# Handing out dense steps by size, and weighing ahead of the parameters, in a fused state-space and dense-layer gradient

## The chip, the cores and the metric

One core of a Trainium2 chip runs the kernel in one launch. The metric is the device time of one execution in microseconds. The kernel before took 776.42 us in the median of three runs (769.07, 776.42, 781.49).

## The reference

A gate `g = sigmoid(u . gate_w)` mixes two branches of a sequence of 2048 rows and 448 channels in bf16. The first is a diagonal state-space model with 256 states in each channel, applied as a long convolution by FFT; the second a dense layer of width 1792 with a squared relu. The kernel returns the mixed output and the gradients of all fourteen parameters.

```python
def _A_ref(u, A_re, A_im, B_re, B_im, C_re, C_im, log_dt, Dskip):
    ...
    P = jnp.exp(logdA[:, :, None] * l[None, None, :])
    K = jnp.einsum("dn,dnl,dn->dl", Cc, P, dB).real
    ...
    Yf = Uf * Kf[None, :, :, :]          # rfft of length 2L of u and K
    y = irfft2(Yf)[..., :L] + u * Dskip
def _B_ref(x, w1, b1, w2, b2):
    h = jnp.einsum("bsd,df->bsf", x, w1) + b1
    r = jnp.where(h > zero, h, zero)
    return jnp.einsum("bsf,fd->bsd", r * r, w2) + b2
g = _sigmoid((x * gate_w).sum(-1, keepdims=True))
out = g * a + (1 - g) * b               # x = u for both branches
_out, _vjp = jax.vjp(_f, ...)           # and the gradients for grad_out
```

## The kernel before

The work goes through these stages. Line numbers are those of the kernel before.

First, input and its gradient G are loaded; U is transposed (L437), and the gate g and 1-g are found (L456 to L461). DA = g G is made (L463). Two first FFT stages (`fwd1`, L236 its matmuls, L210/L211/L220 copies out of PSUM, L244 stores to DRAM) turn U and then DA. Their blocks are staged in a ring of buffers: eight for the first, six for the second, eight blocks each.

Between and behind them stand: the parameters' work on DVE and ACT (L481 to L524: products with dt, an exponential at L512, sines at L519 and L520, a square at L521), which ends in the tables that the chains start from; the weighing DB = (1-g) G (L541, sixteen DVE instructions); the column sum over 1-g (matmuls L544, copy L554); and the gate product, sixteen DVE products DA*U into four slots (L548), each summed by a matmul with ones (L549, copy L551).

Then the second FFT stage. `spectra(q)` (q = 0 to 3) loads a quarter of each of the two transforms (L250), multiplies (`fwd2`, matmuls L260) and stores it (L965). `cmul` (L274 to L279, DVE) multiplies the two, and `inv1` (L296 its matmuls, L300 its stores) begins the way back. Four chains `powers` stand between them: each squares the state's complex factor eleven times over. A level is an ACT copy (L595), an ACT square (L604) and two DVE instructions (L605, L606) that need each other; L591 opens a chain, a store to `rec_d` (L609, on ACT's queue) closes it. The chains use two sets of buffers in turn.

The dense layer runs as a generator of 189 steps that the other stages draw from. `N_(n)` runs the next n steps. A list `cost` gives each a size. A column j of the first layer (14 columns) has four steps: `hidden` of half a column with `turn` (matmuls L661 and L664, relu copies L676, turns L688, squares L689), 24; `mul_1` (L697, copy L703), 19; and again both. After columns 1 and 2 stand four steps each of size 6, `turn_db`: ten transposes (L437), one copy (L710, on ACT for an even number and on DVE for an odd one) into one of two halves of a buffer, and its store (L711, to `DBT_d`). Within `spectra` and `inv1` each slot runs a number of steps: `FW` = (1, 1, 0, 1) behind the four parts of `fwd2`, `IV` = (2, 2) behind the two parts of `inv1`. With four steps run before, forty are done at the end of `spectra` and three `inv1`.

Up to there the order of each engine's instructions is a scheduler's, which may move instructions past one another. From `manual_schedule` on (L972) it is that of the program. There the last `inv1` and the y-tables take ten more steps, and steps are drawn until a product is complete. Then come fourteen periods of the state-space gradient, one for each 32 channels (lists of tokens, `PERIOD`). The token D draws steps until the sum of their sizes reaches an even share of what is left, so that the periods end with six steps left. Stores and loads of the dense layer's later part are held (`defer`) and released at the tokens LY and R, or when a buffer must be used again (`force`); L784 is the copy of the second layer's hidden gradient into one of three such buffers, L794 its store. DMA transposes (L1102) of the y-tables stand in SP's queue between them. A last stage of 148 us, FFTs of the kernel's gradient and the outputs, follows the periods.

Of the kernel before, what the change touches and what calls it, by code (L numbers as in the profile page):

```python
# [23 lines left out]
DT = 4  # L24
# [295 lines left out]
def kernel(ctx, tc, A_u, A_A_re, A_A_im, A_B_re, A_B_im, A_C_re, A_C_im, A_log_dt, A_Dskip,  # L320
# [46 lines left out]
    krow = np.array([p if p < 32 else p // 32 * 32 + (p % 16) * 2 + p // 16 % 2 if p < 64 else 64 + (p % 16) * 4 + p // 16 % 4 for p in range(P)])  # L367
    cs["F1K"] = np.zeros_like(cs["F1BD"])
# [93 lines left out]
    for t in range(LT):  # L462
# [4 lines left out]
             for homes in (((Fs, (0, 1792, 3584, 5376)), (RA, (10752, 12544)), (S1t[0], (0, 1792))), ((S1t[1], (0, 1792, 3584, 5376)), (S1t[0], (3584, 5376))))]  # L467
# [5 lines left out]
    nMI = const.tile([P, 256], bf16, name="nMI")  # L473
    S.mul(nMI[:], ct["MI"][:], -1.0)
    K.nMI = nMI
# [64 lines left out]
    for t in range(LT):  # L540
        V.tensor_scalar(out=DB[:, t, :], in0=G[:, t, :], scalar1=omg32[:, t:t + 1], scalar2=None, op0=ALU.mult)  # L541
    ps = K.ps("S", [P, 512])
    for t in range(LT):
        T_.matmul(ps[0:1, 0:D], lhsT=omg_b[:, t:t + 1], rhs=G[:, t, :], start=(t == 0), stop=(t == LT - 1))  # L544
    psg = K.ps("X", [P, 512])
    gu = K.t("st", [P, 4, D], bufs=2)
    for t in range(LT):
        V.tensor_tensor(out=gu[:, t % 4], in0=DA[:, t], in1=U[:, t], op=ALU.mult)  # L548
        T_.matmul(psg[0:1, 0:D], lhsT=ones_c[:], rhs=gu[:, t % 4], start=(t == 0), stop=(t == LT - 1))  # L549
    row9 = K.t("st", [P, 4, D], bufs=2)  # L550
    S.copy(row9[0:1, 0], psg[0:1, 0:D])  # L551
    G_.dma_start(out_9.rearrange("(o d) -> o d", o=1), row9[0:1, 0])
    row13 = K.t("rec", [1, D])
    S.copy(row13[:], ps[0:1, 0:D])  # L554
    G_.dma_start(out_13.rearrange("(o d) -> o d", o=1), row13[:])
# [59 lines left out]
    w1b = [SB[:, 8192 + 1024 * i:9216 + 1024 * i].rearrange("p (a f) -> p a f", a=DT) for i in range(2)]  # L615
# [33 lines left out]

    def load_w1(jp):  # L650
        b = w1b[jp % 2]
        G_.dma_start(b[:, 0:3], bass.AP(tensor=B_w1.tensor, offset=B_w1.offset + 256 * jp, ap=[[F, P], [P * F, 3], [1, 256]]))
        for h in range(2):
            G_.dma_start(b[64 * h:64 * h + 64, 3], bass.AP(tensor=B_w1.tensor, offset=B_w1.offset + 384 * F + 256 * jp, ap=[[F, 64], [1, 256]]))
# [66 lines left out]
    def first_layer():  # L721

        for jp in range(2):
            load_w1(jp)
# [219 lines left out]

    def D_(want):

        while done < total - TAILN and sum(cost[0:done + 1]) <= want:
            N_(1)
# [741 lines left out]
```

## Time and profile before

| what | value |
|---|---|
| median of three runs | 776.42 us |
| profiled execution, its own time | 771.82 us |
| its span | 769.9 us |
| granted TensorE clock, mean | 0.906 |
| busy: PE, DVE, ACT, POOL | 638.2, 566.7, 510.9, 174.6 us |
| DMA moved | 177.77 MB |

The span is what the profile's times count, from its start; the time of the execution has 1.9 us around it. PE's busy time counts matmuls as they overlap, and those at a lower clock are longer. All durations in the prediction come from this one execution. Where instructions of one engine follow each other without a pause, the profile's duration of one is longer than the distance of their starts, since they overlap; distances are used for sums.

### The profile page before, as it was taken

The numbers are of one execution on the slowest core, as the hardware profiler recorded it, in microseconds if no ns is written. First come the engines' busy times: TensorE is split into PE (matmuls) and PEld (weight loads), VectorE is DVE, ScalarE is ACT, GpSimd is POOL, SyncE is SP. The second block draws the span as 40 slices with busy tenths as digits, with TensorE's granted clock in tenths as the row PEclk, the third lists the DMA queues.
The fourth block names the chain that finished last, engine by engine and source line by source line (L and its number), as shares of the span: only waits on it lengthen the run. The fifth ranks groups of instructions, "written<-read, shape, count | busy, mean of one in ns | idle before, by whom it ended". The sixth has DMA issues, their size and how long they took to land.

```text
span 769.9 us, 20498 instructions
## 1 busy us (share of the span) xinstructions
PE 638.2 (83%) x8597; PEld 339.2 (44%) x8597; DVE 566.7 (74%) x932; ACT 510.9 (66%) x873; POOL 174.6 (23%) x296
## 2 busy tenths in 40 slices
PE   5958968779999888698999997998979987686666
PEld 2412322333456545355665654654636563433211
DVE  1397586775784549598898898698879868859474
ACT  2797958588785746477687677677725544498455
POOL 2152111112174101111211201102100332321543
PEclk9997967899999988889999999999989998799858
DMA  9898586746783995967977977999996976898995
GB/s 206 185 284 255 198 307 240 250 168 217 295 324 90 314 194 128 267 120 206 241 173 206 259 140 194 258 185 251 223 219 129 280 234 206 344 332 303 335 332 146
DMA packets 197115, 177.77 MB, mean 231 GB/s; under 512 B 121534, under 2 KB 174039, under 8 KB 196895
## 3 DMA queue, kind: packets, MB, share of 16 engines
q1 hardware_dynamic: 173823, 113.11, 59.5%
q0 software_dynamic: 15632, 44.48, 18.1%
q10 hardware_dynamic: 7568, 18.88, 6.6%
q8 instruction: 67, 1.10, 0.6%
q14 instruction: 25, 0.20, 0.1%
HBM read 83.95 MB, written 64.32 MB: 193 GB/s over the span
## 4 chain that ended last, share of the span: by engine, by line
PE 50%; ACT 15%; issue 13%; DMA 10%; DVE 7%; POOL 3%; SPq 2%; POOLq 0%; ACTq 0%; DVEq 0%
PE psN L901 9%; PE psN L661 6%; PE psN L697 5%; PE psS L1172 5%; PE psX L1078 4%; DMA U<-in_A_u_dram 3%; PE psF L1140 3%; PE psX L697 2%; PE psN L688 2%; ACT P L1146 2%; DMA hd<-F 2%; PE psN L664 2%; ACT U L689 1%; PE psN L236 1%; ACT S L1121 1%
## 5 line engine op out<-in xcount | busy, mean ns | idle before, releaser
L697 PEld LDWEIGHTS <-U 128*128 128x128 bf16 x448 | 41.5, 101 | 44.7 <-issue 15.7
L1146 ACT CAST P<-psF 128x1024 bf16<-128x1024 f32 x52 | 53.0, 1018 | 8.7 <-PE psF L1140 6.9
L1015 DVE TENSOR_TENSOR F<-Y,F 128x1024 bf16<-128x1024 bf16 (+3 forms) x70 | 47.4, 676 | 13.8 <-ACT F L1043 13.7
L1014 DVE TENSOR_TENSOR Y<-Y,F 128x1024 bf16<-128x1024 bf16 (+3 forms) x70 | 48.0, 685 | 11.1 <-ACT F L1040 7.8
L661 PEld LDWEIGHTS <-S 128*128 128x128 bf16 x336 | 30.9, 102 | 44.5 <-issue 18.7
L697 PE MATMUL psN<-S,U 128*128 128x449 bf16 x224 | 49.9, 366 | 0.0
L1017 DVE TENSOR_TENSOR Y<-Y,F 128x1024 bf16<-128x1024 bf16 (+3 forms) x70 | 48.1, 688 | 2.4
L661 PE MATMUL psN<-S 128*128 128x512 bf16 x168 | 46.3, 401 | 1.3 <-ACT U L676 1.1
L1140 PE MATMUL psF<-S,R 41*128 41x32 bf16 x1664 | 29.7, 175 | 14.1 <-ACT P L1146 12.3
L1179 POOL DMA_DIRECT2D s_d<-st x28 | 16.0, 579 | 105.1 <-ACT st L1177 87.0
L1140 PEld LDWEIGHTS <-R 41*128 41x128 bf16 x1792 | 27.5, 94 | 26.1 <-issue 23.5
L901 PEld LDWEIGHTS <-U 128*128 128x128 bf16 x252 | 24.5, 102 | 33.0 <-issue 9.8
L697 PE MATMUL psX<-D,U 128*128 128x448 bf16 x160 | 37.3, 370 | 2.0 <-ACT D L703 2.0
L689 ACT ACTIVATE U<-psN 128x1024 bf16<-128x1024 bf16 x35 | 36.2, 1033 | 0.0
L661 PE MATMUL psN<-K,S 128*128 128x512 bf16 x126 | 35.2, 410 | 0.7 <-ACT P L784 0.7
L901 PE MATMUL psN<-S,U 128*128 128x448 bf16 x140 | 30.5, 367 | 6.0 <-DMA S<-in_B_w_dram 4.7
L676 ACT ACTIVATE U<-psN,b_f 128x512 bf16<-128x512 f32 x48 | 31.1, 688 | 6.0 <-PE psN L664 4.3
L296 PEld LDWEIGHTS <-cb_MI 64*128 64x128 bf16 x256 | 15.2, 95 | 31.6 <-issue 22.3
L901 PE MATMUL psN<-D,U 128*128 128x448 bf16 x112 | 26.1, 390 | 2.7 <-ACT U L889 2.7
L1172 PEld LDWEIGHTS <-M 128*64 128x64 bf16 x896 | 25.8, 110 | 5.0 <-issue 3.1
L1172 PE MATMUL psS<-ident,P 128*64 128x128 bf16 x896 | 27.4, 219 | 0.0
L784 ACT ACTIVATE P<-psN 128x512 bf16<-128x512 f32 x20 | 10.9, 598 | 23.7 <-PE psN L664 15.2
(416 smaller groups left out, 1695.4 us busy)
## 6 DMA issues: line engine op xcount, KB each, us to landing
sp<-K ACTq DMA_DIRECT2D x8, 896.0 KB, 4.1
rT_d<-U POOLq DMA_DIRECT2D x11, 512.0 KB, 3.0
hd<-F SPq DMA_DIRECT2D x11, 448.0 KB, 14.0
U<-rT_d SPq DMA_DIRECT2D x9, 512.0 KB, 5.9
X<-gd SPq DMA_DIRECT2D x5, 896.0 KB
U<-dhT_d SPq DMA_DIRECT2D x5, 896.0 KB, 16.1
rec_d<-F ACTq DMA_DIRECT2D x2, 1920.0 KB
hd<-st ACTq DMA_DIRECT2D x8, 448.0 KB, 4.7
```

Of the source, the lines that this page charges most:

```text
L661: T_.matmul(pss[k][:], lhsT=w[:, dt], rhs=x(2 * half + k)[:, dt], start=(dt == 0), stop=False, skip_group_check=True)
L676: S.activation(r[:, 512 * lb:512 * lb + 512], pss[k][:], ACT.Relu, bias=b1_f[:, j:j + 1])
L689: S.activation(hn[j % 2][:, 8 * th:8 * th + 8, :], ps[:], f)
L697: T_.matmul(ps[:, 0:w], lhsT=hn[j % 2][:, t, :], rhs=rhs[:, t, :], start=(t == 0), stop=(t == LT - 1))
L901: T_.matmul(ps[:, 0:D], lhsT=src[j][:, P * x:P * x + P], rhs=ws[:, j, :], start=(j == 0), stop=(j == FT - 1))
L1014: V.tensor_tensor(out=run(yb, dst, [64, X2], [d0[1], n // d0[1]], [1, d0[1]]), in0=run(yb, 0, [64, X2], *src), in1=pr, op=ALU.mult)
L1015: V.tensor_tensor(out=run(vb, 0, [n, X2], [d0[1], n // d0[1]], [1, d0[1]]), in0=run(yb, 0, [64, X2], *src), in1=pi, op=ALU.mult)
L1017: return V.tensor_tensor(out=hi, in0=hi, in1=run(vb, n, [2 * n, W2], [-n, 2], [1, n]), op=ALU.add)
L1078: T_.matmul(ps[32 * g:32 * g + 32, i], lhsT=run(xb, 2048 * (1 - t) + w, [W2, 32]), rhs=Y[:, w, t, 0:NY], start=(h == 0 and t == 0), stop=( ...
L1140: T_.matmul(psz[t][:, 32 * b:32 * b + 32], lhsT=yt[64 * t:64 * t + NY, b, :], rhs=DKc[64 * t:64 * t + NY, c % 2, 16 * (j % 2) + b].rearran ...
L1146: S.copy(run(zbs[c, h][:, 0:1], 16 * (j % 2), [1024, 2], [64, NA], [32, 2], [1, 16]), run(psF[:, 0, 0:1], 0, [512, 2], [1, NA], [NA, 2], [ ...
L1172: T_.matmul(sps[64 * h:64 * h + 64, cc, r, :], lhsT=Q[h][r][:, 1024 * t + 64 * a:1024 * t + 64 * a + 64], rhs=(nident if r == 0 and t == 1 ...
```

## The change

1. `F_(n)` takes the place of `N_(n)` within `spectra` and the first three `inv1`: each slot adds n times `UNIT` = 20 to a share, and steps run until the sizes of all steps behind the first four reach it. With 36 slots the share ends at 720. By the list of sizes 44 steps are then done.
2. The weighing, the column sum and the gate product stand ahead of the parameters' work.
3. `nMI` is a constant loaded by DMA and no longer made by ACT.
4. The first two pairs of columns of w1 are loaded on SP's queue ahead of the parameters' work, where they were loaded on POOL's queue at the start of the first layer.
5. The second transform's staging ring has eight buffers: two lie in the place of G, which the weighing and the column sum have read by then.

```diff
+    cs["nMI"] = -cs["MI"]
...
-             for homes in (..., ((S1t[1], (0, 1792, 3584, 5376)), (S1t[0], (3584, 5376))))]
+             for homes in (..., ((S1t[1], (0, 1792, 3584, 5376)), (S1t[0], (3584, 5376)), (GD.rearrange("p k t d -> p (k t d)"), (0, 1792))))]
     K.fwd1(lambda j: U[:, j, 0:D], gd[0], stage[0], 5)
     load_const("M2", nc.sync)
     load_const("MI", nc.sync)
...
-    nMI = const.tile([P, 256], bf16, name="nMI")
-    S.mul(nMI[:], ct["MI"][:], -1.0)
-    K.nMI = nMI
+    load_const("nMI", nc.sync)
+    K.nMI = ct["nMI"]
+    w1b = [...]
+
+    def load_w1(jp, q=G_):
+        b = w1b[jp % 2]
+        q.dma_start(b[:, 0:3], ...)
+        for h in range(2):
+            q.dma_start(b[64 * h:64 * h + 64, 3], ...)
+
+    for jp in range(2):
+        load_w1(jp, nc.sync)
+    for t in range(LT):
+        V.tensor_scalar(out=DB[:, t, :], in0=G[:, t, :], scalar1=omg32[:, t:t + 1], scalar2=None, op0=ALU.mult)
+    ps = K.ps("S", [P, 512])
+    for t in range(LT):
+        T_.matmul(ps[0:1, 0:D], lhsT=omg_b[:, t:t + 1], rhs=G[:, t, :], start=(t == 0), stop=(t == LT - 1))
+    psg = K.ps("X", [P, 512])
+    gu = K.t("st", [P, 4, D], bufs=2)
+    for t in range(LT):
+        V.tensor_tensor(out=gu[:, t % 4], in0=DA[:, t], in1=U[:, t], op=ALU.mult)
+        T_.matmul(psg[0:1, 0:D], lhsT=ones_c[:], rhs=gu[:, t % 4], start=(t == 0), stop=(t == LT - 1))
+    row9 = ...
     W0 = K.t("P14", [P, 7168])
...
-    for t in range(LT):
-        V.tensor_scalar(out=DB[:, t, :], ...)
...
-        for jp in range(2):
-            load_w1(jp)
         for half in range(2):
             hidden(0, half)
...
+    share = 0
+
+    def F_(n):
+
+        nonlocal share
+        share += n * UNIT
+        while sum(cost[4:done]) < share:
+            N_(1)
+
...
-            K.fwd2(s1, q, sp, lambda ii: N_(FW[ii]))
+            K.fwd2(s1, q, sp, lambda ii: F_(FW[ii]))
...
-    FW, IV = (1, 1, 0, 1), (2, 2)
+    FW, IV, UNIT = (1, 1, 0, 1), (2, 2), 20
...
-        K.inv1(Pc, q, hd[0], between=lambda q2: N_(IV[q2]))
+        K.inv1(Pc, q, hd[0], between=lambda q2: F_(IV[q2]))
```

More of the change, by code (lines that the diff above doesn't have):

```diff
@@ L466 @@
     stage = [[b[:, o:o + 1792].rearrange("p (a d) -> p a d", d=D) for b, os_ in homes for o in os_]
-             for homes in (((Fs, (0, 1792, 3584, 5376)), (RA, (10752, 12544)), (S1t[0], (0, 1792))), ((S1t[1], (0, 1792, 3584, 5376)), (S1t[0], (3584, 5376))))]
+             for homes in (((Fs, (0, 1792, 3584, 5376)), (RA, (10752, 12544)), (S1t[0], (0, 1792))), ((S1t[1], (0, 1792, 3584, 5376)), (S1t[0], (3584, 5376)), (GD.rearrange("p k t d -> p (k t d)"), (0, 1792))))]
     K.fwd1(lambda j: U[:, j, 0:D], gd[0], stage[0], 5)
@@ L472 @@
     K.M2 = [ct["M2"][:, 1024 * q:1024 * q + 1024] for q in range(4)]
-    nMI = const.tile([P, 256], bf16, name="nMI")
-    S.mul(nMI[:], ct["MI"][:], -1.0)
-    K.nMI = nMI
+    load_const("nMI", nc.sync)
+    K.nMI = ct["nMI"]
+    w1b = [SB[:, 8192 + 1024 * i:9216 + 1024 * i].rearrange("p (a f) -> p a f", a=DT) for i in range(2)]
+    def load_w1(jp, q=G_):
+        b = w1b[jp % 2]
+        q.dma_start(b[:, 0:3], bass.AP(tensor=B_w1.tensor, offset=B_w1.offset + 256 * jp, ap=[[F, P], [P * F, 3], [1, 256]]))
+        for h in range(2):
+            q.dma_start(b[64 * h:64 * h + 64, 3], bass.AP(tensor=B_w1.tensor, offset=B_w1.offset + 384 * F + 256 * jp, ap=[[F, 64], [1, 256]]))
+    for jp in range(2):
[10 more added lines that the diff above has]
+        T_.matmul(psg[0:1, 0:D], lhsT=ones_c[:], rhs=gu[:, t % 4], start=(t == 0), stop=(t == LT - 1))
+    row9 = K.t("st", [P, 4, D], bufs=2)
+    S.copy(row9[0:1, 0], psg[0:1, 0:D])
+    G_.dma_start(out_9.rearrange("(o d) -> o d", o=1), row9[0:1, 0])
+    row13 = K.t("rec", [1, D])
+    S.copy(row13[:], ps[0:1, 0:D])
+    G_.dma_start(out_13.rearrange("(o d) -> o d", o=1), row13[:])
     W0 = K.t("P14", [P, 7168])
@@ L538 @@
     nc.sync.dma_start(b2_bc[:], B_b2.partition_broadcast(P))
-    for t in range(LT):
[L541 to L555, printed above, removed]
     K.pairs = 2
@@ L614 @@
     hn = [hv[:, 4096 + 2048 * i:6144 + 2048 * i].rearrange("p (t f) -> p t f", f=P) for i in range(2)]
-    w1b = [SB[:, 8192 + 1024 * i:9216 + 1024 * i].rearrange("p (a f) -> p a f", a=DT) for i in range(2)]
     dw2s = DBx[:, 7168:8064].rearrange("p (k d) -> p k d", k=2)
@@ L648, in rows_of @@
         return bass.AP(tensor=tensor, offset=j * P * L, ap=[[L, P], [1, L]])
[L650 to L654, printed above, removed]
     def wide(half, w, x):
```

## The prediction

> **What bounds the kernel now.** I read first the busy times by stretch, cut where the stages change; columns: stretch, its length, PE, weight loads, DVE, ACT and POOL busy (with instruction counts), granted clock, DMA share, GB/s.
>
> ```profile
> core 0: us, PE busy (x) PEld busy (x) DVE busy (x) ACT busy (x) POOL busy (x), PEclk, DMA share, GB/s
> ...
> 41.00:75.00 34.00, 21.64 (x82) 5.84 (x80) 29.70 (x78) 26.77 (x47) 13.18 (x24) 0.80 0.93 290
> 75.00:101.00 26.00, 24.64 (x157) 10.16 (x157) 16.52 (x34) 22.80 (x40) 5.05 (x9) 1.00 0.47 170
> 101.00:129.00 28.00, 18.61 (x79) 6.31 (x78) 21.16 (x44) 20.21 (x35) 4.89 (x8) 0.59 0.74 273
> 129.00:141.00 12.00, 8.93 (x62) 3.68 (x61) 7.59 (x13) 4.83 (x8) 1.44 (x2) 0.93 1.02 371
> 141.00:213.00 72.00, 63.21 (x375) 26.24 (x375) 49.34 (x104) 57.39 (x108) 11.69 (x20) 0.94 0.59 219
> 213.00:239.00 26.00, 24.33 (x378) 15.62 (x380) 23.44 (x33) 18.65 (x30) 15.50 (x15) 1.00 0.66 244
> 239.00:280.00 41.00, 36.19 (x462) 19.38 (x456) 19.35 (x29) 27.59 (x42) 12.30 (x22) 0.88 0.91 238
> 280.00:622.00 342.00, 305.53 (x5801) 188.88 (x5802) 287.96 (x401) 223.63 (x361) 48.95 (x83) 0.95 0.93 207
> ```
>
> From 280 to 622 us PE is busy 305.5 of 342: PE work put there is paid nearly whole. From 41 to 213 no engine is full. PE has 137 of 172 us, part of it at a clock of 0.59, and ACT 132. What ends each wait there is ACT and DVE handing each other the levels of the four parameter chains (L595 to L606), with dense work between them on ACT, in order. The worst stretch is 101 to 141: PE busy 27.5 of 40, ACT 25.0. The timelines of ACT, DVE and PE show where the change will touch; each row is start, duration, instruction, and in brackets the idle time before it with what ended it.
>
> ```profile
> 51.74 0.95 ACT L512 ACTIVATE P<-R 128x896 f32<-128x896 f32 x1 [0.70 <-DVE R L510]
> ...
> 69.66 0.53 ACT L210 CAST K<-psN 128x448 bf16<-128x448 f32 x1 [3.99 <-DVE st L548]
> ...
> 129.93 0.91 ACT L220 CAST st<-psF 128x896 bf16<-128x896 f32 x1
> 132.15 1.01 ACT L710 COPY S<-psS 128x1024 bf16<-128x1024 bf16 x1 [1.31 <-PE psS L437]
> ...
> 134.25 0.53 ACT L210 CAST st<-psN 128x448 bf16<-128x448 f32 x1 [1.08 <-PE psF L296]
> 134.68 0.62 ACT L591 COPY F<-P 128x512 bf16<-128x512 bf16 x1
> 135.19 0.62 ACT L595 CAST F<-P 128x512 bf16<-128x512 f32 x1
> ...
> 140.10 1.01 ACT L710 COPY S<-psS 128x1024 bf16<-128x1024 bf16 x1 [4.29 <-DMA DBT_d<-S]
> 141.01 0.63 ACT L604 ACTIVATE P<-P 128x512 f32<-128x512 f32 x1
> ```
>
> ```profile
> 65.07 0.39 DVE L548 TENSOR_TENSOR st<-K,U 128x448 bf16<-128x448 bf16 x1 [0.92 <-PE psX L549]
> ...
> 69.55 0.42 DVE L605 SCALAR_TENSOR_TENSOR R<-P 128x256 f32<-128x256 f32 x1
> ```
>
> ```profile
> 58.23 0.53 PE L236 MATMUL psN<-K,cb_F1BD 128*128 128x448 bf16 x1 [6.78 <-ACT Y L210]
> ```
>
> To see: the exponential L512 waits for the parameter products on DVE. The first spectrum copy at 69.66 waits for the last gate product. From 129.9 to 141.0 ACT idles 1.31+1.08+4.29 us before turned-gradient copies (L710), and the third chain's first square (L604, 141.01) stands behind the last of these. DVE does the first chain's first L605 only at 69.55, behind twelve gate products. PE lost 6.78 us before 58.23 to staging buffers in use.
>
> **The change, part by part.** Durations are gaps between starts, where work runs back to back.
>
> *A. Four dense steps leave the loop.* The order of instructions in the changed program has 42 relu copies (L676) ahead of the last inverse store of this stage, against 38; step counts are 44 against 40. The steps are one column of the first layer, two halves. A half in the loop:
>
> ```profile
> 241.08 0.62 PE L688 MATMUL psN<-ident,U 128*128 128x128 bf16 x8
> 241.53 1.68 PE L697 MATMUL psN<-D,U 128*128 128x448 bf16 x8
> 243.05 1.46 PE L661 MATMUL psN<-S 128*128 128x512 bf16 x6
> 244.44 0.39 PE L664 MATMUL psN<-S 64*128 64x512 bf16 x2
> ```
>
> L661+L664 from 243.05 to 244.76 (1.71), L688 0.45, L697 1.52: 3.7 us a half, 7.4 in two. They leave the stretch 239 to 280, where PE is busy 36.2 of 41 (0.88): 7.4 x 0.88 = **-6.5 us**, by the bounds 0 and -7.4.
>
> *B. The same four steps enter the stretch 41 to 213.* On PE that is 7.4 us into 35 us of idle time. On ACT: four L676 at 0.58, two L689 at 0.91, one L703 at 0.42 = 4.6 us into 40 us of idle time, of which 15 lie in 101 to 141, where the new order has most of them (two relus and one turn more before the second chain's store, two and one more before the third chain). Bounds 0 (all hidden) and +4.6 (ACT on the path throughout); ACT is busy 0.77 of the stretch. I take **+2**.
>
> *C. Turned-gradient steps.* Eight cheap steps (10 transposes, a copy, a store) used to count as whole slots; by size a slot takes three of them. In the new order all four ACT copies stand before the second chain's store, so the 6.7 us of idle time between 129.9 and 141.0 go: -6.7. But they come closer together: between an ACT copy and the next but one, which needs the same half of the buffer, there are two chain levels, at 1.8 us each (L605 starts at 154.28, 156.34, 157.98). The store takes 5.3 us in the median from issue to landing (2.7 to 6.6), plus 0.7 of issue. So 6.0-3.6 = 2.4 us of new wait on ACT, twice: +4.8. Behind a waiting copy stand the next L595/L604, hence the chain. Bounds -6.7 and +2 (two waits of 4.3, the one measured). I take **-1.9**.
>
> *D. Weighing and gate products ahead of the parameters.* DVE: sixteen L541 at 0.257 (eleven in 2.83) and sixteen L548 at 0.32 (four in 1.28) = 9.2 us before L502, which began at 41.21. So the product that releases L512 ends near 61 instead of 51.7. In the new order ACT has L512 ahead of the first relu: with the two extra stage buffers the first transform's copies end near 55.5 (six of its eight blocks are copied from 40.41 to 51.05, so two more need 3.5 us, plus about 1 for gate matmuls between them; before, 62.4), then ACT idles to 61. Then L512, four relus, two small copies, L591, a table load, two sines, the square and the last four relus and two turns, to about 73.5, where the first chain's square runs; it ran at 63.49. But DVE's first level began at 69.55 and its second square at 72.81; the new second square comes near 77: the chain is 4 to 5 us late. Against that, the first four dense steps end at 73.5 instead of 80.75. In ACT work done by 75 us the two orders are level: ahead by four relus and two turns (4.1 us); behind by two pieces of the first chain, three of the second and two spectrum copies (3.8). Bounds -6 (dense lead kept) and +5 (chain lag kept). I take **0**.
>
> *E. Small edits.* nMI comes by DMA: 0.31 us less on ACT, off a full stretch, counted nothing. Six loads of w1 move from POOL's queue (3.9 us of issue at 52 to 57) to SP's, ahead of the transform's stores: SP's first L244 of that transform moves from 43.93 to about 48.5 and its eight stores at 0.65 still keep up with copies that end at 55.5. Were that cover gone, the second spectrum's load would be 2 us late; PE first uses it at 91.19. POOL is free earlier. Price 0.
>
> The loop's later order (held stores, transposes on SP) shifts by up to two steps in a period; the wait for a held store (ACT 8.5 us before 322.82) keeps its cause, since the fourth L784 still comes before a release. Price 0, either way up to 8.
>
> **Sum:** -6.5+2-1.9+0 = **-6.4 us**. The profiled execution took 771.82 (span 769.9): 765.4. It lies 4.6 below the median of the runs, 776.42: by that 770.0. I say **767**, between them.
>
> [...]
>
> **Rivals.**
> 1. *The chain's late start decides (slower).* ACT stands behind L512, and the four chains in series, not ACT's total, set the stage's end: D +5, B +4.6, C 0, A -6.5: **+3.1**, 775 to 780. For it: L595 waits 12.7 us in total for L606. Against: ACT's pauses of 101 to 141 are room for a late chain. It decides if the second chain's store is issued after about 133 (129.08 before).
> 2. *The gaps close (faster).* B 0, C -6.7, D -4, A -7.4: **-18**, 753 to 758. For it: at 101 to 129 PE is granted 0.59, and three L661 take 1.44 us at 116.48 against 0.81 at 156.47; work without gaps would run at the second price. Against: ACT, not PE, ends most waits there. [...]
> 3. *The loop gives nothing back.* Its first periods end in waits for DMAs (8.5 us before 322.82), so A 0: **0**, 771 to 776.
>
> **Chances.** Forecast 0.45, first rival 0.2, second 0.2, third 0.15. The range leaves out the far halves of both outer rivals' spreads: **752 to 781**. A measurement of this kernel tells about 2% from no change (15.5 us): faster by more needs below 761, which is the second rival and an edge of the forecast: **0.21**; slower by more needs 792, only with the first rival and a worse loop: **0.05**; within: **0.74**.
>
> **What would show it.** No wait of 6.8 us before the first transform's last matmuls; L512 near 61 with ACT idle before it; first L605 near 71; two waits of some 2 us before L710 instead of one of 4.3; less than 6 us from the second chain's store to the third chain's square; the last inverse store near 212 as before; the end of the period loop about 6.5 us earlier. I am wrong if the store of the second chain or the last inverse store moves by more than 5 us, or if the loop from 239 keeps its length.

## The result, and the profile after

The changed kernel takes 797.73 us in the median of four runs (795.24 to 803.56), the kernel before 774.63 in the runs beside it. The ratio is 1.0326, with an interval of 1.0274 to 1.0377: slower by 3.3%. I had forecast 767. The profiled execution took 797.16 us against 771.82, its span is 795.4 against 769.9: 25.5 us more.

Three places in the span tell where they lie. The first turning of the y-tables (L1113 before, L1123 after), which I call the end of the stage, moved from 227.4 to 238.0 us: +10.5. From there to the start of the last product that makes kernel rows (L1078, L1088), which I call the periods, it took 402.3 us instead of 392.0: +10.3. The rest took 155.1 instead of 150.4: +4.7. Nothing was gained in any of the three.

The busy times of the changed kernel by stretch, for the stretches shown of before, and then the periods, cut some 12 and 20 us later than there because the same work begins and ends so much later (columns: stretch, length, PE, weight loads, DVE, ACT, POOL, granted clock, DMA share, GB/s):

```profile
core 0: us, PE busy (x) PEld busy (x) DVE busy (x) ACT busy (x) POOL busy (x), PEclk, DMA share, GB/s
41.00:75.00 34.00, 22.95 (x93) 7.34 (x91) 26.39 (x69) 24.18 (x42) 10.17 (x19) 0.90 0.96 295
75.00:101.00 26.00, 22.75 (x151) 10.20 (x152) 20.00 (x43) 22.67 (x40) 4.93 (x8) 1.00 0.51 186
101.00:129.00 28.00, 21.40 (x117) 8.74 (x119) 20.81 (x43) 21.50 (x37) 5.80 (x9) 0.76 0.78 274
129.00:141.00 12.00, 7.45 (x40) 3.41 (x39) 6.03 (x13) 8.10 (x13) 1.98 (x3) 0.69 0.72 270
141.00:213.00 72.00, 61.58 (x329) 24.25 (x332) 45.51 (x93) 53.96 (x101) 10.56 (x19) 0.89 0.57 209
...
251.00:292.00 41.00, 31.57 (x448) 17.01 (x445) 17.20 (x24) 25.67 (x40) 11.07 (x20) 0.88 0.93 244
292.00:642.00 350.00, 297.02 (x5732) 186.46 (x5759) 289.15 (x407) 220.62 (x356) 47.76 (x83) 0.94 0.91 201
```

From 101 to 141 ACT is busy 29.6 of 40 us, where it had been 25.0: the heaped steps did fill some of its pauses. From 141 to 213 it is busy 54.0 instead of 57.4: new pauses stand there. From 251 on, PE is less busy than before in stretches that are as long or longer (31.6 of 41 against 36.2; 297 of 350 against 305.5 of 342). Of these 13.1 us less, 7.4 are the four steps that left.

The timeline of ACT in the changed kernel, the rows that answer to those of before (start, duration, instruction, idle time before it and what ended it; most lines have moved: the exponential is L538, the turned-gradient copy L713, relu L679):

```profile
61.72 0.95 ACT L538 ACTIVATE P<-R 128x896 f32<-128x896 f32 x1 [5.22 <-DVE R L536]
...
130.09 1.01 ACT L713 COPY S<-psS 128x1024 bf16<-128x1024 bf16 x1 [2.48 <-DMA DBT_d<-S]
...
136.30 0.38 ACTq L619 DMA_DIRECT2D rec_d<-R  x1
...
138.50 0.69 ACT L679 ACTIVATE U<-psN,b_f 128x512 bf16<-128x512 f32 x1
144.88 0.37 ACTq L300 DMA_DIRECT2D hd<-st  x1
145.29 0.69 ACT L679 ACTIVATE U<-psN,b_f 128x512 bf16<-128x512 f32 x1 [6.10 <-issue]
...
176.20 0.54 ACT L210 CAST st<-psN 128x448 bf16<-128x448 f32 x1
184.09 0.69 ACT L679 ACTIVATE U<-psN,b_f 128x512 bf16<-128x512 f32 x1 [7.34 <-PE psN L667]
```

To see: the exponential is at 61.72, as the prediction said, and the two waits for the turned gradient's stores are there (3.18 us before the copy at 104.46, 2.48 at 130.09). The second chain's store is issued at 136.30 instead of 129.08, and the last inverse store at 221.5 instead of 212.4. From the second chain's store to the third chain's first square (147.81) it still takes 11.5 us, where it took 11.9. Two pauses of 6 and 7 us are new. Up to 144.88 ACT's queue stands at the issue of an inverse's store, whose data a DVE copy brings only at 144.8, and behind it stands a relu. From 176.7 to 184.1 a relu waits for PE, whose queue has parts of the spectrum ahead of it that go to and fro with DVE copies.

### The profile page after: what moved, and what is told of

The parts are those of the page before. It is cut to its first block, busy times and chain, and to the rows that moved or that the text cites. A ratio compares the mean times of both kernels' runs of the same rounds, so it can differ in the third digit from the quotient of the medians.

```text
span 795.4 us, 20464 instructions
## 1 busy us (share of the span) xinstructions
PE 635.1 (80%) x8555; PEld 342.7 (43%) x8597; DVE 567.8 (71%) x932; ACT 510.0 (64%) x872; POOL 168.7 (21%) x291
## 4 chain that ended last, share of the span: by engine, by line
PE 43%; DVE 14%; ACT 14%; DMA 13%; issue 12%; POOL 2%; SPq 1%; ACTq 0%; POOLq 0%; DVEq 0%
PE psN L902 9%; PE psN L664 5%; PE psS L1182 4%; PE psX L1088 3%; PE psN L700 3%; DMA R<-Y 3%; DMA U<-in_A_u_dram 2%; PE psF L1150 2%; DMA hd<-F 2%; PE psX L700 2%; DVE Y L1024 2%; PE psN L236 1%; DVE F L1025 1%; ACT U L692 1%; PE psN L667 1%
## 5 line engine op out<-in xcount | busy, mean ns | idle before, releaser
L1156 ACT CAST P<-psF 128x1024 bf16<-128x1024 f32 x52 | 53.1, 1022 | 18.2 <-PE psF L1150 17.8
L679 ACT ACTIVATE U<-psN,b_f 128x512 bf16<-128x512 f32 x52 | 34.2, 690 | 21.8 <-PE psN L667 13.8
L700 PE MATMUL psN<-S,U 128*128 128x449 bf16 x224 | 48.1, 356 | 0.0
L902 PE MATMUL psN<-S,U 128*128 128x448 bf16 x140 | 33.2, 391 | 10.8 <-DMA S<-in_B_w_dram 5.6
L1150 PE MATMUL psF<-S,R 41*128 41x32 bf16 x1664 | 29.8, 175 | 12.8 <-ACT P L1156 7.4
L700 PE MATMUL psX<-D,U 128*128 128x448 bf16 x176 | 39.4, 364 | 0.5 <-ACT D L706 0.5
L1150 PEld LDWEIGHTS <-R 41*128 41x128 bf16 x1792 | 27.3, 93 | 26.6 <-issue 23.6
L692 ACT ACTIVATE U<-psN 128x1024 bf16<-128x1024 bf16 x33 | 34.1, 1033 | 2.1 <-PE psN L691 2.1
L664 PE MATMUL psN<-K,S 128*128 128x512 bf16 x99 | 30.0, 420 | 4.6 <-issue 4.0
L1065 DVE COPY Y<-rec 128x256 bf16<-128x256 bf16 x14 | 11.9, 849 | 23.2 <-DMA R<-Y 19.7
```

Of the source, the lines that this page charges most:

```text
L664: T_.matmul(pss[k][:], lhsT=w[:, dt], rhs=x(2 * half + k)[:, dt], start=(dt == 0), stop=False, skip_group_check=True)
L679: S.activation(r[:, 512 * lb:512 * lb + 512], pss[k][:], ACT.Relu, bias=b1_f[:, j:j + 1])
L692: S.activation(hn[j % 2][:, 8 * th:8 * th + 8, :], ps[:], f)
L700: T_.matmul(ps[:, 0:w], lhsT=hn[j % 2][:, t, :], rhs=rhs[:, t, :], start=(t == 0), stop=(t == LT - 1))
L902: T_.matmul(ps[:, 0:D], lhsT=src[j][:, P * x:P * x + P], rhs=ws[:, j, :], start=(j == 0), stop=(j == FT - 1))
L1150: T_.matmul(psz[t][:, 32 * b:32 * b + 32], lhsT=yt[64 * t:64 * t + NY, b, :], rhs=DKc[64 * t:64 * t + NY, c % 2, 16 * (j % 2) + b].rearran ...
```

## The experiments

All readings are of single executions, in us. The same program's stage, executed in two kernels, ended at 238.0 and 238.7, and in another pair at 226.9 and 230.7; seven kernels with the periods' order of before took 389.7 to 396.8 for the periods. So differences below some 4 us in the stage of one execution, and below some 7 in its periods, mean little, and the ratios, from several executions, decide. Three profiled executions lie far from the median of their kernel: size40's (782.58 against 788.19) and after_all's (769.26 against 778.86) were the fastest of theirs, aligned's (793.36 against 787.81) the slowest.

| kernel | second chain's store | end of stage | periods | last ACT copy to end of span | ratio to before (interval) |
|---|---|---|---|---|---|
| before | 129.1 | 227.4 | 392.0 | 5.5 | |
| after | 136.3 | 238.0 | 402.3 | 10.9 | 1.0326 (1.0274 to 1.0377) |
| size44 | 131.8 | 234.1 | 399.9 | 5.5 | 1.0273 (1.0187 to 1.0359) |
| size40 | 128.8 | 236.4 | 394.7 | 5.5 | 1.0197 (1.0123 to 1.0270) |
| moves_number | 129.0 | 227.1 | 389.7 | 10.7 | 1.0067 (1.0032 to 1.0102) |
| after_size40 | 128.8 | 230.2 | 396.8 | 10.8 | 1.0211 (1.0144 to 1.0279) |
| moves_pool | 129.5 | 229.0 | 395.3 | 5.5 | 0.9996 (0.9962 to 1.0030) |
| pairs44 | 133.5 | 233.7 | 402.5 | 10.9 | 1.0241 (1.0185 to 1.0297) |
| aligned | 135.2 | 238.7 | 397.2 | 10.9 | 1.0184 (1.0122 to 1.0245) |
| halves4 | 130.5 | 233.0 | 402.3 | 10.9 | 1.0230 (1.0176 to 1.0284) |
| after_all | 122.2 | 226.9 | 389.9 | 5.5 | 1.0027 (0.9988 to 1.0065) |
| all_but_aligned | 127.1 | 230.7 | 407.6 | 5.5 | 1.0202 (1.0151 to 1.0253) |
| before_halves4 | 130.3 | 225.2 | 395.3 | 5.5 | 0.9962 (0.9928 to 0.9997) |
| pool_halves4 | 125.2 | 223.3 | 395.4 | 5.5 | 0.9994 (0.9954 to 1.0034) |

### Which part costs: size or moves

My first theory was that the moved weighing delays the chains and so the stage, and that the four extra steps disturb the periods. Four kernels separate the hand-out (by number 40, by size 40, by size 44) from the moves.

The first is the kernel before with the hand-out by size alone:

```diff
-            K.fwd2(s1, q, sp, lambda ii: N_(FW[ii]))
+            K.fwd2(s1, q, sp, lambda ii: F_(FW[ii]))
-    FW, IV = (1, 1, 0, 1), (2, 2)
+    FW, IV, UNIT = (1, 1, 0, 1), (2, 2), 20
-        K.inv1(Pc, q, hd[0], between=lambda q2: N_(IV[q2]))
+        K.inv1(Pc, q, hd[0], between=lambda q2: F_(IV[q2]))
```

> The kernel before, with the dense steps of the second FFT stage handed out by size (unit 20, 44 steps done) and nothing else changed: weighing, gate product, nMI, loads of w1 and staging buffers stay as before. Measured places: the first turning of the y-tables (end of the stage; before 227.4 us, after 238.0) and the last product that makes kernel rows in the periods (before 619.5, after 640.4). Theory 1 (the moved weighing makes the chains late, and the loop is disturbed by the four extra steps): the stage ends near 227 to 230, the periods from there take 400 us or more instead of 392, time +6 to +12 against before. Theory 2 (the extra dense steps in the stage are what makes the stage late): the stage ends near 235 to 238, time +15 to +25. My prediction's steps A to C, if only the moves were misjudged: stage 227, periods 386, time -6.

The ratio was 1.0273. The stage ended 6.7 us late and the periods took 7.9 us more. So both theories had a half: hand-out and four steps by themselves make the stage late and the periods longer.

The second is that kernel with `UNIT = 18`:

> The kernel before, with the dense steps of the stage handed out by size but with unit 18, so that 40 steps are done at its end as before; the program is that of before from the period loop on. Theory 1 (the four extra steps disturb the loop): the periods keep 392 us, and the stage ends between 221 and 229, since the cheap turned-gradient steps are packed: time -6 to +2. Theory 2 (giving out by size itself, with its packed copies and their waits for stores, delays the chains): the stage ends at 231 to 235, time +4 to +8.

The ratio was 1.0197, worse than either theory gave. The periods kept their length (394.7), as theory 1 said, but the stage ended 9.0 us late without a single extra step, and no sooner than with 44. So the way of handing out makes the stage late by itself. From 75 to 236 us ACT was busy 116.8 us (before, from 75 to 227: 117.7); its idle time there rose from 34.3 to 44.2. The chief parts of that idle time are 8.6 us of waits for stores of the turned gradient and 11.4 us for PE's turns (two waits of 5.4 and 6.0).

The third is the changed kernel with the hand-out by number:

```diff
-            K.fwd2(s1, q, sp, lambda ii: F_(FW[ii]))
+            K.fwd2(s1, q, sp, lambda ii: N_(FW[ii]))
-        K.inv1(Pc, q, hd[0], between=lambda q2: F_(IV[q2]))
+        K.inv1(Pc, q, hd[0], between=lambda q2: N_(IV[q2]))
```

> The changed kernel with the steps handed out by number as before (40 steps): weighing and gate product ahead of the parameters' work, nMI by DMA, loads of w1 on SP's queue and eight staging buffers stay. Theory 1 (the moves make the chains late): the exponential of the parameters runs near 61 us instead of 51.7, the first chain's store near 106 instead of 101.5, the stage ends at 233 to 238, the periods keep 392 us, time +6 to +11. Theory 2 (the moves cost nothing, the share by size does): first store near 101, stage 227, time -2 to +2.

Theory 1 fell. The exponential did come late (61.24) and the first chain's store too (105.1 instead of 101.5), but the second chain's store came at 129.0 and the stage ended at 227.1, both as before. What the moves cost, 0.7%, stood at the very end: 10.7 us instead of 5.5 between ACT's last copy and the end of the span.

The fourth is the changed kernel with `UNIT = 18`:

> The changed kernel with unit 18 instead of 20, so that 40 steps are done at the end of the stage, the same number as before. Theory 1 (moves make the stage late by some 8, the four extra steps make the loop longer by some 8 and the tail by 5): stage ends near 235, periods 392, time +8 to +12 against before. Theory 2 (the loop is longer because it starts late, or by the moves, not by the four steps): periods stay near 402 and the tail at 153, time +20 to +25.

The ratio was 1.0211. Here the stage ended 2.8 us late, and no copy waited for a store of the turned gradient; in size40, with the same slots, two copies waited 8.6 us in all. So the same hand-out shows in other waits as the scheduler's order round it falls. By the ratios it costs about as much with the moves (1.0211 against 1.0067) as without them (1.0197); where the time goes with them, the one execution does not show.

### The last five microseconds

ACT's last copy in moves_number ends at 763.4, and the output's stores are through by 767. From there to the end at 774, the DMA view shows a single packet:

```profile
DMA packets 1, 0.01 MB, mean 1 GB/s; under 512 B 0, under 2 KB 0, under 8 KB 0
## 3 DMA queue, kind: packets, MB, share of 16 engines
q14 instruction: 1, 0.01, 0.5%
```

It is on a queue of kind "instruction". The kernel before has no such packet there. Over its whole span that queue has 25 packets, 0.20 MB, and over that of the changed kernel 26, 0.21 MB. The moves had put seven DMAs more on SP's queue, so I put them back on POOL's, in the kernel moves_number:

```diff
-    load_const("nMI", nc.sync)
+    load_const("nMI", G_)
-        load_w1(jp, nc.sync)
+        load_w1(jp)
```

> The kernel with the moves and steps by number (40), but with the loads of nMI and of the first two pairs of columns of w1 on POOL's queue instead of SP's. With them on SP's queue all three kernels that have the moves end 10.7 to 10.9 us after their last copy (before: 5.6), and in that time the trace shows a single packet of 8 KB on an instruction queue, which the kernels without the moves don't have there. Theory 1 (the seven DMAs more on SP lengthen SP's program so that one more piece of it is fetched at its very end): the gap from the last copy to the end of the span falls back to 5.5, the time is about 5 us below that of the same kernel with SP's loads: 770 to 774, ratio to before 0.995 to 1.000. Theory 2 (another engine's program, or the moves as such): the gap stays near 10.7 and the ratio at 1.007.

The gap and the time came out as theory 1 gave them: the gap was 5.5, the packet was gone, and the ratio went from 1.0067 to 0.9996, 5 us. So the queue of the seven DMAs is the cause. The way that theory 1 gave is not shown: no row says whose program the packet belongs to. What lasts in the gap is an instruction of POOL at the end of the program, a DRAIN, and the last instructions of all other engines follow it (their last DRAINs start at 769.3 to 769.4 us in the kernel before, 0.5 to 0.6 before the end of the span, and at 794.9 in the changed one, 0.5 before it). It is the longest of the three DRAINs in these rows, first of moves_number, then of moves_pool (least, median and longest duration in ns; first and last start in us):

```profile
L1695 POOLq DRAIN  x3: 46/108/9390, 764.0 to 773.9; - x3
```

```profile
L1695 POOLq DRAIN  x3: 46/108/4192, 769.2 to 773.9; - x3
```

The long DRAIN takes 9.4 to 9.6 us in the six kernels with these loads on SP's queue and 4.2 in the eight others. In moves_number it ends at 773.36, while SP's last work of its own is done at 767.08, before the packet at 768.1. In aligned the gap is as long, and such a packet comes only 0.5 us behind the end of the span. Why POOL's DRAIN lasts longer when those loads stand on SP's queue stays open.

moves_pool speaks also to the first rival. In its execution the first chain was later than in any other (timeline of ACT):

```profile
63.57 0.95 ACT L538 ACTIVATE P<-R 128x896 f32<-128x896 f32 x1
...
113.19 0.38 ACTq L619 DMA_DIRECT2D rec_d<-F  x1
...
129.50 0.38 ACTq L619 DMA_DIRECT2D rec_d<-R  x1
...
213.93 0.37 ACTq L300 DMA_DIRECT2D hd<-st  x1
```

The first store is 11.7 us late, the second 0.4, the last inverse store 1.5 (before: 101.5, 129.1, 212.4). A late first chain is taken up before the second ends.

### What makes the stage late

By the list of sizes, the slots hold these steps (a star where cheap ones are among them). The four numbers of a spectrum are its parts, the two of an inverse its halves:

```
            spectra 0            spectra 1            inverse 0  spectra 2           inverse 1  spectra 3           inverse 2
by number   1/1/0/1  1/1/0/1*    1*/1*/0/1* 1/1/0/1   2*/2*      1*/1/0/1 1/1/0/1    2/2        1/1/0/1 1/1/0/1    2/2
unit 20     2/0/0/1  1/1/0/3*    2*/1/0/1   1/1*/0/4* 1/2        1/1/0/1  1/1/0/1    2/1        1/1/0/1 1/1/0/1    2/2
unit 18     1/1/0/1  1/1/0/1*    3*/1/0/1   1/1/0/1*  4*/2       0/1/0/1  1/1/0/1    1/2        1/1/0/1 0/1/0/1    2/1
pairs       1/1/0/1  1/1/0/2*    2*/1/0/1   1/1/0/2*  3*/2       1/1/0/1  1/1/0/1    2/2        1/1/0/1 1/1/0/1    2/2
```

A full step of 19 or 24 overshoots a share of 20 or 18, so some slots get fewer steps than by number and others up to four. To try this, the changed kernel got a regular rule with the same 44 steps (the last row; one slot of it still holds three steps, two of them cheap):

```diff
-        share += n * UNIT
-        while sum(cost[4:done]) < share:
-            N_(1)
+        for _ in range(n):
+            c = cost[done]
+            N_(1)
+            if c == 6 and cost[done] == 6:
+                N_(1)
```

> The changed kernel with the slots filled by a regular rule instead of by size: each slot runs one step, and where that is a cheap turned-gradient step and the next is cheap too, both; 44 steps are done at the end of the stage as in the changed kernel, but no slot is empty and none has three or four steps. Theory 1 (handing out by size leaves slots empty and heaps steps in others, so that ACT's queue runs dry or stands behind the store of an inverse for 6 to 7 us twice): first turning of the y-tables near 230 to 232 instead of 238, time 5 to 8 us below the changed kernel. Theory 2 (four more steps and the late first chain are ACT work on the path, 7.6 us of it between 75 us and the end of the stage): the stage ends at 236 to 239, time as the changed kernel within 2 us.

The stage ended at 233.7, 4.3 us earlier, and the ratio fell to 1.0241 (6.6 us less). The pause of 7.3 us near 184 shrank to 2.2; one of 6.7 stayed near 143. By the ratio the time is theory 1's; the stage's end lies between the two theories: the rule takes away part of the delay.

The other suspect was the wait for the turned gradient's stores. The changed kernel got four pieces of buffer:

```diff
+        b = DBTs[:, :, 256 * (k % 2):256 * (k % 2) + 256] if k % 4 < 2 else S1t[k % 2][:, 7168:8192].rearrange("p (a l) -> p a l", a=DT)
-        (S.copy if k % 2 == 0 else V.tensor_copy)(DBTs[:, :, 256 * (k % 2):256 * (k % 2) + 256], ps[:])
+        (S.copy if k % 2 == 0 else V.tensor_copy)(b, ps[:])
-        G_.dma_start(bass.AP(tensor=DBT_d, ...), DBTs[:, :, 256 * (k % 2):256 * (k % 2) + 256])
+        G_.dma_start(bass.AP(tensor=DBT_d, ...), b)
```

> The changed kernel with four instead of two pieces of buffer for the turned gradient (two more in room that nothing uses in this stage), so that no copy waits for the store of the copy before the last. It takes away the waits of 3.2 and 2.5 us for those stores on ACT. Theory 1 (these waits are on the path): second chain's store 4 to 6 us earlier (136.3 in the changed kernel), stage ends at 232 to 234, time 4 to 6 us below the changed kernel. Theory 2 (what was a wait becomes a later stall, since the end of the stage is set by ACT's work and by stalls behind it): store up to 6 earlier but the stage ends within 2 us of 238.

Theory 1 held: the second chain's store came 5.8 us earlier, the stage ended 5.0 earlier, and the ratio fell to 1.0230 (7.4 us less). A wait of ACT in the first half of this stage is paid at its end; the two long pauses behind it kept their places (6.41 and 7.34 us).

### What makes the periods longer

The number that the periods' shares are worked out from was set back to that of before:

```diff
-    base, goal = sum(cost[0:done]), sum(cost[0:total - TAILN])
+    base, goal = sum(cost[0:done - 4]), sum(cost[0:total - TAILN])
```

> The changed kernel with one number changed: the shares of dense steps in the periods are worked out from the step that the kernel before had reached at the start of the periods (51), so the first four shares of the first period are already done, and from step 60 on every period draws the steps that it drew before, with the releases and transposes on SP's queue in the order of before. Theory 1 (the loop is longer because the steps' new places against the releases put the transposes of the y-tables behind or beside the held loads): no wait for a transpose (19.7 us before the y-table's seeds in the changed kernel) and from the first turning of the y-tables to the last product that makes kernel rows 384 to 392 us instead of 402, time 10 to 18 us below the changed kernel. Theory 2 (the loop is longer for another reason, as its late start or the clock): 398 us or more, time as the changed kernel within 4 us.

The ratio fell from 1.0326 to 1.0184, 11 us, as theory 1 gave; in the profiled execution, the slowest of this kernel, the periods were only 5.1 us shorter, at 397.2, and DVE's waits for transposes had shrunk from 19.7 to 12.3 us, not gone. So I put all four repairs together, and then took this one away again.

> The changed kernel with four repairs at once: regular slots with pairs of cheap steps (44 steps), four pieces of buffer for the turned gradient, shares of the periods worked out from step 51, and the loads of nMI and w1 on POOL's queue. Alone, the first three gave 4.3 us (end of the stage 233.7), 5.0 us (233.0) and 5.1 us (periods 397.2), the last 5.2 us (gap at the end 5.5). Theory 1 (the causes are separate): the stage ends at 228 to 230, the periods take 395 to 398, the rest 150: span 773 to 778, ratio to before 1.000 to 1.006; the four steps that left the periods still gain nothing, since the first period waits some 6 us for the step sums' way through DRAM. Theory 2 (regular slots and more buffer take away the same stalls, and ACT's 7.6 us more of work are the rest): the stage ends at 232 to 234, span 778 to 783, ratio 1.008 to 1.014.

> The kernel with the four repairs, less one: the shares of the periods are again worked out from the step reached (55), as in the changed kernel; regular slots, four pieces of buffer and POOL's loads stay. In single executions the time from the first turning of the y-tables to the last product for kernel rows lay between 389.7 and 396.8 in the seven kernels whose periods follow the order of before from step 51 and at 399.9 to 402.5 in the four with shares from step 55. Theory 1 (the place of the steps against the releases of held stores and loads costs 6 to 10 us by itself): the stage ends at 226 to 229, the periods take 399 to 403, ratio to before 1.010 to 1.016 (1.0027 with the repair). Theory 2 (the periods were longer because they began late, or because of the stage's order): periods 390 to 396, ratio 1.001 to 1.005.

With all four the ratio is 1.0027, no longer told from 1: together the four causes make up the loss. Alone they gave 6.6, 7.4, 11 and 5 us by the ratios, 30 in all, while together they take 23 off the loss, so some 7 us are overlap or scatter. Without the aligned shares it is 1.0202: 13.5 us for one number in a formula, more than theory 1 gave. In both pairs the stage before the periods is the same program, and the periods differ only in which steps fall into which period. Over all fourteen kernels, the nine with shares from step 51 took 389.7 to 397.2 us for the periods, the five with shares from step 55 took 399.9 to 407.6.

SP's queue shows what that does to the order there. A period's four transposes of the y-tables (L1112; L1102 in before) stand in it between held stores (L796; L794) and loads (L774 and L777; L772 and L775) of the dense layer. The timeline of SP's queue, first of before, then of the kernel with all repairs, then of that without the aligned shares, round the third period's transposes (start, time from the first of the row's instructions to the end of its last, instruction):

```profile
302.67 12.23 SPq L1102 DMA_TRANSPOSE R<-Y  x4
314.95 0.57 SPq L775 DMA_DIRECT2D K<-rT_d  x1
...
319.44 0.70 SPq L794 DMA_DIRECT2D dhT_d<-R  x1
```

```profile
303.19 10.92 SPq L1112 DMA_TRANSPOSE R<-Y  x4
314.17 0.62 SPq L777 DMA_DIRECT2D K<-rT_d  x1
...
319.33 0.44 SPq L796 DMA_DIRECT2D dhT_d<-R  x1
```

```profile
293.03 0.53 SPq L777 DMA_DIRECT2D K<-rT_d  x1
...
308.82 0.32 SPq L774 DMA_DIRECT2D U<-rT_d  x1
309.24 0.38 SPq L796 DMA_DIRECT2D dhT_d<-R  x1
309.71 15.09 SPq L1112 DMA_TRANSPOSE R<-Y  x4
```

In the first two the seven held transfers go out behind the third period's transposes. In the last they go out ahead of them, the last two (a load and a store of 512 KB each) in the microsecond before, and the four transposes take 15.1 us instead of 10.9 to 12.2. DVE, which writes the next y-table over the one that is being transposed (L1065, L1055 before), waits for the transposes 5.5 us in the periods before, 19.7 in the changed kernel, 25.4 without the aligned shares and 13.1 with all repairs (aligned alone: 12.3). These waits alone do not decide: in halves4, with shares from step 55 too, they come to 8.5 us, and its periods take 402.3.

One wait can be followed through all kernels. In the ninth period a square of the dense layer (L891) needs rows that a held load (L879) brings, and this load stands in SP's queue behind the period's transposes. The rows of SP and ACT, first without the aligned shares, then with all repairs:

```profile
485.66 11.00 SPq L1112 DMA_TRANSPOSE R<-Y  x4
497.01 0.54 SPq L879 DMA_DIRECT2D S<-rT_d  x1
...
503.81 1.70 ACT L891 ACTIVATE S<-S 128x1792 bf16<-128x1792 bf16 x1 [6.99 <-DMA S<-rT_d]
```

```profile
474.01 12.20 SPq L1112 DMA_TRANSPOSE R<-Y  x4
...
487.15 0.36 SPq L879 DMA_DIRECT2D S<-rT_d  x1
...
494.89 1.70 ACT L891 ACTIVATE S<-S 128x1792 bf16<-128x1792 bf16 x1 [1.98 <-DMA S<-rT_d]
```

In every kernel the load goes out 5 to 8 us behind the start of the period's first product for kernel rows. Where the steps run ahead, their square is reached sooner and waits: 6.3 to 8.7 us in the five kernels with shares from step 55, 1.1 to 2.4 in the nine others. From this product to the next period's it takes 30.4 to 32.6 us in the five and 24.7 to 26.0 in the nine.

PE's own waits in the periods, without the aligned shares and then with all repairs (what waited and for what; total us, times, longest; L903 and L813 are L901 and L811 of before):

```profile
PE psN L903 <- DMA U<-dhT_d: 7.9, 2, 5.2
PE psX L1088 <- DVE Y L1027: 7.0, 2, 3.9
...
PE psN L903 <- ACT S L891: 5.2, 2, 2.8
PE psN L903 <- ACT U L891: 4.9, 1, 4.9
PE psN L813 <- ACT U L692: 4.5, 3, 1.7
```

```profile
PE psF L1150 <- DVE S L1135: 5.8, 1, 5.8
...
PE psX L1088 <- DVE Y L1027: 5.0, 1, 5.0
...
PE psN L903 <- ACT U L891: 2.7, 1, 2.7
PE psN L903 <- DMA U<-dhT_d: 1.9, 1, 1.9
...
PE psN L813 <- ACT U L692: 1.4, 3, 0.6
...
PE psN L903 <- ACT S L891: 1.0, 1, 1.0
```

The five of the first list come to 29.5 us; the same five with all repairs come to 12.0. Other rows go the other way (L1150 for ACT's L1156: 5.4 against 11.6). There is no single large wait: loads, buffers and hand-overs are each late by a few us, in the first layer as in the last products. From the first product for kernel rows to the last, PE is idle 66 of 399 us in the first and 57 of 381 in the second; the rest of the difference is PE's busy time, 333 against 324 us for the same matmuls at a granted clock of 0.92 against 0.95. The second execution was the fastest of its kernel, so these two lie 18 us apart in the periods, where the ratios give 13.5. Beyond the ninth period's wait, some 6 us, it stays open which of these waits begets which.

### The steps that left

In the changed kernel the four steps do not leave one place: the shares are worked out anew, so the first period runs eight steps instead of nine, the steps are three ahead at the end of each of the first three periods, and the lead is gone at the end of the thirteenth. With the aligned shares the four steps leave the first period and no other. The first row of the second list shows what came in their place, and so do the timelines of PE and ACT in the kernel with all repairs:

```profile
249.99 1.68 PE L700 MATMUL psN<-D,U 128*128 128x448 bf16 x8
257.50 0.61 PE L1150 MATMUL psF<-S,R 41*128 41x32 bf16 x32 [5.83 <-DVE S L1135]
```

```profile
255.94 1.05 ACT L1131 COPY S<-K 128x512 bf16<-128x512 bf16 x1 [4.12 <-DMA K<-dk_d]
```

and the chain that ended last in the same stretch, up to that instruction:

```profile
248.15 3.67 DMA K<-dk_d
...
255.94 1.06 ACT S L1131
...
257.02 0.44 DVE S L1135
...
257.50 0.63 PE psF L1150 x25
```

The step sums go to DRAM (`dk_d`), come back turned, and are spread by ACT (L1131) and weighed by DVE (L1135) before PE can go on. In the kernel before, ACT came to its copy at 257.97 straight from dense work, the same DVE instruction ran at 259.06, and PE waited 1.6 us for it. The dense steps had covered that way. Taken out, 7.4 us of them shortened this period from 26.5 to 24.3 us (24.9 in aligned).

### Two candidates

The four pieces of buffer were tried on the kernel before, and on the kernel with the moves and POOL's loads.

> The kernel before with four pieces of buffer for the turned gradient and nothing else changed. In before one such store is waited for, 4.3 us on ACT ahead of the third chain's first square, with 1.3 us for PE ahead of the copy before. Theory 1 (a wait on ACT in this stage is paid at its end): the stage ends at 223 to 225 instead of 227.4 and the time falls by 2.5 to 4.5 us, ratio 0.994 to 0.997. Theory 2 (the order is the same and the wait is covered, or its place is taken by the next): stage 226 to 228, ratio 0.998 to 1.002.

> The kernel with the moves, steps by number, nMI and w1 loaded on POOL's queue, and four pieces of buffer for the turned gradient. Theory 1 (waits for the turned gradient's stores are on the path): stage ends 3 to 5 us before 228.9, time 2 to 5 us below the same kernel with two pieces (ratio 0.9996 to before), so 0.994 to 0.997. Theory 2: 0.998 to 1.002.

On the kernel before the ratio is 0.9962 (0.9928 to 0.9997): some 3 us, the one version faster than both kernels, by a little more than the runs leave uncertain. With the moves it is 0.9994, and the 5.7 us that its profiled stage shows (223.3 against 229.0) are not found in the times. Against the kernel before with four pieces too, the one with all repairs is 0.65% slower, 5 us, about what the runs leave uncertain.

## Why the prediction was wrong

**What bounds the kernel.** The sentence that failed is "PE work put there is paid nearly whole". A stretch with PE busy at 0.88 was read as PE's. The first period ends by a way through DRAM that the dense work covers, and in the ninth a held load sets the pace as soon as the steps run ahead of it.

**A, -6.5.** It was 2 us at best. With the order kept, the first period gave back 2.2 of 7.4, since PE then waits 5.8 for the step sums. The work that I took away was itself the cover of another way. The term also let all four steps leave the stretch 239 to 280; the changed kernel's shares spread them over the periods, and its first period took 26.9 us. The third rival, that the loop gives nothing back, had this right; its 771 to 776 has no loss in it.

**B, +2.** Not clearly at fault. With regular slots and enough buffer the stage of 44 steps ended at 226.9 and 230.7, against 225.2 for 40 steps with the same buffer and 223.3 with the moves as well: +1.7 to +7.4 in single executions, of bounds 0 to 4.6.

**C, -1.9.** The waits were right (3.18 and 2.48 for two of 2.4), and so was their mechanism. The -6.7 beside them was wrong. Of it, 1.08 stood before an inverse's copy (L210) and not before a turned gradient's. The time from the second chain's store to the third chain's first square, which was to fall below 6 us, stayed at 11.5: filling those pauses did not bring the third chain nearer. The uneven slots left two pauses of 6.1 and 7.3 us elsewhere, which no term had, and the second chain's store moved by 7.2 us. The condition I had set for the first rival (a store after 133) was met, but not by its cause.

**D, 0.** Right, within its bounds. L538 ran at 61.72 (said: 61), the first chain's square at 77.73 (73.5), DVE's first level at 75.05 (71), and moves_number and moves_pool show that nothing of this reaches the end of the stage. The first rival, that the chains' late start decides, is refuted. Of the second, that the gaps close, a part came: from 101 to 129 us the granted clock rose from 0.59 to 0.76. But it fell from 0.93 to 0.69 and from 0.94 to 0.89 in the next two stretches, and no time was gained. That work without gaps would run at the lower of the two prices named there was my estimate, and no row shows that the gaps set the clock. In the kernel before, L661 took 1.44 us at 116.48 at a granted clock of 0.50 (115 to 118 us) and 0.81 at 156.47 at one of 1.00 (155 to 158); PE was busy 2.26 us of the first 3 and 2.11 of the second, so the gaps were no smaller where the clock was full. PE's longest wait from 85 to 213 us was 2.6 us.

**E, 0, "either way up to 8".** The wait of 6.8 us before the first transform's last matmuls is gone, as said, though PE waits 6.5 us before 64.40 for the first spectrum's load in its place. Two terms were missed. The loads on SP's queue cost 5 us at the end of the program. And the remark on the loop's later order was the largest term of all: 11 to 13.5 us, beyond its bound, and all of it a loss. I had priced it at nothing because one wait for a held store was to keep its cause. It did not keep its place: the 8.5 us before 322.82 became 3.8 before 365.4 and 4.1 before 394.7, a period later. And I had not followed the other held loads and stores: steps that run ahead, by up to three and not two, reach the ninth period's load too soon.

**What stood behind a wait on ACT** started after it in both kernels: in the kernel before, the square at 141.01 behind a copy that waits 4.29 us for a store (140.10); in the changed kernel, at 145.29 a relu behind the store's issue at 144.88, after 6.10 us without work. I had weighed such waits for the chains only, and the price fell on the dense steps behind a store.

**Sum.** Stage +10.5, periods +10.3, end +4.7 against my 2 - 1.9, -6.5 and 0.

## What to carry to other kernels

Before taking covering work out of a stretch in which one engine looks full, find the longest way through other engines and DRAM in it: what is left of that way is the new length. When work that is drawn by shares starts from another point, compare, from there to the end, when each held load and store goes out with when its step needs it, since one number there cost 13.5 us. Handing out by size does not even out a queue if the pieces are as large as the shares; a regular pattern, and more buffer behind it, each did better here.

## What the runs showed of the hardware

The queue that some early loads stand on cost 5 us at the very end of this program. In the six kernels with the loads of nMI and w1 on SP's queue the gap from the last ACT copy to the end of the span was 10.7 to 10.9 us, in the other eight 5.5. Moving the seven DMAs to POOL's queue took the difference away. In the gap POOL's DRAIN lasts 9.4 to 9.6 us against 4.2, and the last DRAINs of the other engines start behind it (at 794.9 of 795.4 us in the changed kernel). What makes it longer is not shown: in moves_number SP's last work was done at 767.08, before the one instruction packet of the gap came at 768.1, and in aligned no packet lies in the gap.

Four transposes by DMA took 21.8 us in the second period of the kernel before and 12.2 and 10.9 in the third and fourth. Over all fourteen kernels the second period's took 21.5 to 24.8; the third's took 10.7 to 12.2 in the nine kernels with shares from step 51 and 15.1 to 16.6 in the five where held loads go out just ahead of them. Why stays open.
